# Retention and a bilinear feed-forward on one core: the last 512 rows reordered, with PSUM banks of their own and four-batch rows stored by one DMA

## The chip, the cores and the metric

The kernel runs on one core of a Trainium2 chip. That core has TensorE (PE in the profile, with its weight loads as PEld), VectorE (DVE), ScalarE (ACT), GpSimd (POOL) and SyncE (SP), and 16 DMA engines that SP, ACT and POOL can give work to. PSUM, where TensorE writes its products, is used here in banks of 128 x 512 numbers of 32 bits. The metric is the time of one execution on the device, in microseconds (us). The kernel before took 321.82 us (median of three runs, 321.82 to 322.19).

## The reference, cut to what matters

Two stages are chained. The first is a retention layer (attention with a decay instead of a softmax) over 8 batches, 8 heads, 576 positions and 64 numbers a head:

```
scores = scale * np.matmul(q, k.transpose(0, 1, 3, 2))
Dmat = np.where(rel >= 0, gamma[:, None, None] ** rel[None, :, :], 0.0)
x = np.matmul(scores * Dmat, v)      # then heads side by side: (4608, 512)
```

The second takes these 4608 rows of 512 through a bilinear feed-forward with 1536 inner columns:

```
a = x @ w_a
b = x @ w_b
out = a * b @ w_out                  # (4608, 512), float32
```

## The kernel before

The 4608 rows are cut into 18 groups of 256 (`NP = 18`), and these into blocks of 512, 256, 256 and then 512 rows. For each block `ffn_block` (L1064) runs the three products of the feed-forward: for each of 12 chunks F of 128 inner columns, four matmuls with `w_a` (L1090), a copy by ACT (`ha`, L1101), four matmuls with `w_b` (L1108) and a multiplication by DVE into `hT` (L1113). The work of the retention for later groups is spread between these matmuls from a list that is sorted by due time (`todo`); in the last block nothing of it is left.

From group 6 on the third product is not made directly. `rows_mixed` (L982) makes it by a seven-product scheme for 2 x 2 blocks (in the manner of Strassen and Winograd): the 256 rows of a group are taken as two halves, and so are the inner columns and the 512 output columns. Sums of the weights' blocks are made once (`wo_sums`); sums of the rows' blocks are made by DVE as `hT` comes (`row_sums`, L944, called after F = 7 and after F = 11). A product is six matmuls of 128 x 256, one per pair of chunks, 12 pairs of chunks halved to `NP2 = 6`. `product(g, way, ps)` issues those of one way (1 to 7), group g (0 or 1 of the block) and pairs ps. Per block that is 2 x 7 x 6 = 84 matmuls at L1009.

The results are put together like this, per group, with the lines of the profile:

- Ways 3 and 4 go to the two halves of a bank, `straights[g]`. ACT copies them to `straight` (`kept`, L1019).
- Way 1 goes to half of a bank, `both[:, g]`, which the two groups share.
- Ways 5 and 2 go to the halves of `crosses[g]`. ACT copies them to `crossed` (L1019); POOL adds `crossed` and `straight` into the two middle quarters of the group's result `osb` (L1038); DVE makes `less` = way 1 - `crossed` (L1045).
- Ways 7 and 6 are added on top of 4 and 3 in `straights[g]`; DVE adds `less` to each half, which gives the first and the last quarter of `osb` (L1054).

The order in which this is written out is the order on each engine. Before the change it is: 3 and 4 for both groups (the last pair of chunks at the end), the two copies, way 1 for both groups, ways 5 and 2 for group 0 and then for group 1, each with its copy, sum and `less`, then ways 7 and 6 for group 0 with its two additions, then the same for group 1.

A row of `osb` holds two rows of the output, so that one partition's row of 1024 numbers is 4 KB in one piece of the output. `store_mixed` (L959) issues the stores (L972). Of the twelve groups that go this way, ten lie in one batch each: one DMA of 128 partitions. Two groups (`LEFT`) are made of the last 64 positions of four batches each: four DMAs of 32 partitions, one per batch. In all blocks but the last, the stores are kept in `formed` and issued by SP when the next block has come to F = 2 (L1099). In the last block, group 0 is one of the two four-batch groups and group 1 lies in one batch. Group 1 is stored in three pieces by SP: the middle two quarters after POOL's sum, then the first and the last quarter after DVE's additions. Group 0 is stored whole, by four DMAs from ACT's queue, after its two additions.

PSUM has eight banks here: four in the pool `ps_ffn`, two in `ps_sc` and two (one tile) in `ps_o`. A new tile of a pool waits until the readers of the tile that had its place are done.

Of the kernel before, what the change touches and what calls it, by code (L numbers as in the profile page):

```python
# [10 lines left out]
FP32 = mybir.dt.float32  # L11
# [3 lines left out]
ALU = mybir.AluOpType  # L15
# [3 lines left out]
def kernel(  # L19
# [10 lines left out]
    nc = tc.nc  # L30

    B, H, S, D = q.shape
# [12 lines left out]
    NP = NTOK // 256  # L45
    LEFT = {NP - 3: 0, NP - 1: 1}
# [15 lines left out]
    def place(n):  # L62
        return n if n < NP - 2 else 2 * NP - 3 - n

    def rows_of(n):

        if n not in LEFT:
            b, m = PAIRS[n]
            return [(kp, 0, 128, b, 256 * m + 128 * kp) for kp in (0, 1)]
        return [(i // 2, 64 * (i % 2), 64, 4 * LEFT[n] + i, S - 64)  # L70
                for i in range(4)]

    def pool(name, bufs, space=None):
        kw = {} if space is None else {"space": space}
        return ctx.enter_context(tc.tile_pool(name=name, bufs=bufs, **kw))
# [13 lines left out]
    late, early = {}, ExitStack()  # L89
# [13 lines left out]
    ps_ffn = pool("ps_ffn", 4, PS)  # L103
    opening, ps_sc, ps_o = ExitStack(), {}, {}
# [94 lines left out]
    for a in (0, 1):  # L199
        nc.gpsimd.affine_select(  # L200
            out=mask_s[64 * a:64 * a + 64], in_=mask_s[64 * a:64 * a + 64],
# [58 lines left out]
    def pair_tables(step):  # L260
# [6 lines left out]
        else:  # L267
            for h in (2 * step - 2, 2 * step - 1):
# [8 lines left out]
                for n in range(FIRST)]  # L277
    second = sum_pool.tile([128, FIRST, HP, 64], FP32, tag="sums",
                           name="second")
# [28 lines left out]
    def work(budget, up_to=2):  # L308
        jobs.sort(key=lambda job: job[0])
        while jobs and jobs[0][0] <= up_to and jobs[0][1] <= budget:  # L310
            _, cost, job = jobs.pop(0)
            job()
            budget -= cost

    def pass_on(count):
        while copies_due and count:
            copies_due.pop(0)()
            count -= 1
# [610 lines left out]
    WIDE = DM // 2  # L929
# [29 lines left out]
    def store_mixed(G, osb, cols=slice(0, 2 * DM), on=nc.sync):  # L959

        n = place(G)
        for kp, r0, m, b, s0 in rows_of(n):
            if n in LEFT:
                p0 = kp * 64 + r0 // 2
                m //= 2
            elif kp == 1:
                continue
            else:
                p0, m = 0, 128
            rows = out[b * S + s0:b * S + s0 + 2 * m].rearrange(  # L970
                "(p two) c -> p (two c)", two=2)
            on.dma_start(rows[:, cols],  # L972
                              osb[p0:p0 + m].rearrange("p k c -> p (k c)")
                              [:, cols])

    formed = []

    def store_formed():
        while formed:
            store_mixed(*formed.pop(0))  # L980

    def rows_mixed(tok0, hT, sums):  # L982

        pass_on(math.inf)
        NP2 = NF // 2
        pair = [tok0 // 256 + g for g in (0, 1)]
        closing = NP - 1 in pair
        straights = [ps_ffn.tile([128, 2, WIDE], FP32, tag="ab",
                                 name=f"m34{g}") for g in (0, 1)]
        mixed = ps_o[0].tile([128, 2, 2, WIDE], FP32, tag="o", name="m15")  # L990
        apart = ps_ffn.tile([128, 2, WIDE], FP32, tag="ab", name="m52")
        both, crosses = mixed[:, 0], (mixed[:, 1], apart)

        def product(g, way, ps, begins=True):
            t0 = 256 * g
            to = {1: both[:, g], 2: crosses[g][:, 1], 3: straights[g][:, 0],
                  4: straights[g][:, 1], 5: crosses[g][:, 0],
                  6: straights[g][:, 0], 7: straights[g][:, 1]}[way]
            for p in ps:
                even, odd = 2 * p, 2 * p + 1  # L1000
                rows, cols = {
                    1: (sums[:, 0, p, g], wo_sums[:, 0, p]),
                    2: (hT[:, even, t0 + 128:t0 + 256], wo_sb[:, even, 0:WIDE]),
                    3: (hT[:, even, t0:t0 + 128], wo_sums[:, 3, p]),
                    4: (hT[:, odd, t0 + 128:t0 + 256], wo_sums[:, 4, p]),
                    5: (hT[:, odd, t0:t0 + 128], wo_sb[:, odd, WIDE:]),
                    6: (sums[:, 1, p, g], wo_sums[:, 1, p]),
                    7: (sums[:, 2, p, g], wo_sums[:, 2, p])}[way]
                nc.tensor.matmul(to, rows, cols, start=(begins and p == 0),  # L1009
                                 stop=True, skip_group_check=True)  # L1010
                yield 0.5, False

        osbs = [o_pool.tile([128, 2, DM], FP32, tag="osb", name="osb2")
                for _ in pair]
        flats = [osb.rearrange("p k m -> p (k m)") for osb in osbs]

        def kept(name, own):
            t = late[name].tile([128, 2, WIDE], FP32, tag=name, name=name)
            nc.scalar.copy(t, own)  # L1019
            return t  # L1020

        first, rest = range(NP2 - 1), (NP2 - 1,)
        for part in (first, rest):
            for g in (0, 1):
                yield from product(g, 3, part)
                yield from product(g, 4, part, False)
        kept_straight = [kept("straight", straights[g]) for g in (0, 1)]
        for part in (range(4), range(4, NP2)):
            for g in (0, 1):
                yield from product(g, 1, part, g == 0)  # L1030
        work(math.inf)
        pass_on(math.inf)
        lesses = []
        for g in (0, 1):
            yield from product(g, 5, range(NP2))
            yield from product(g, 2, range(NP2), False)
            crossed = kept("crossed", crosses[g])
            nc.gpsimd.tensor_tensor(  # L1038
                flats[g][:, WIDE:3 * WIDE].rearrange("p (k m) -> p k m", k=2),
                crossed, kept_straight[g], op=ALU.add)  # L1040
            if pair[g] == NP - 1:
                store_mixed(pair[g], osbs[g], slice(WIDE, 3 * WIDE))
            less = late["less"].tile([128, 2, WIDE], FP32, tag="less",
                                     name="less")
            nc.vector.tensor_tensor(  # L1045
                less, both[:, g].unsqueeze(1).to_broadcast([128, 2, WIDE]),
                crossed, op=ALU.subtract)
            lesses.append(less)
        for g in (0, 1):
            yield from product(g, 7, range(NP2), False)  # L1050
            yield from product(g, 6, range(NP2), False)
            for k, at, i in ((1, slice(0, WIDE), 0),
                             (0, slice(3 * WIDE, 4 * WIDE), 1)):
                nc.vector.tensor_tensor(flats[g][:, at], straights[g][:, k],  # L1054
                                        lesses[g][:, i], op=ALU.add)
                if pair[g] == NP - 1:
                    store_mixed(pair[g], osbs[g], at)
            if closing and pair[g] < NP - 1:
                store_mixed(pair[g], osbs[g], on=nc.scalar)
            elif not closing:  # L1060
                formed.append((pair[g], osbs[g]))
        yield 0, True

    def ffn_block(tb, tok0, n, runs):  # L1064
# [62 lines left out]
        if tok0 >= 256 * MIXED:  # L1127
            yield from rows_mixed(tok0, hT, sums)
            return
# [119 lines left out]
    starts, at = {}, 0.0  # L1249
# [89 lines left out]
    at = 0.0  # L1339
# [40 lines left out]
```

## Time and profile before

| what | value |
|---|---|
| median of three runs | 321.82 us |
| the profiled execution | 322.96 us, of which the span from first to last instruction is 321.0 us |
| granted TensorE clock, mean | 0.995 |
| TensorE busy | 312.6 us, 97% of the span |
| DVE, ACT, POOL busy | 62%, 45%, 49% |
| products of the last block, L1009 | 305.8 to 315.2 us |
| stores issued after 314.5 us | three by SP, four by ACT, 1.05 MB |
| the one DMA of 128 rows issued by SP at 314.6 | landed 2.2 us later |
| of the seven stores, the longest from issue to landing | 3.6 us |

The profile is one execution, and its span is counted from the first instruction. A line of a group names the source line, the engine, the operation, and `output<-inputs` with the tiles' names; a name such as SPq or ACTq is that engine's queue of instructions that issue DMAs. In the DMA answers q1 is SP's queue and q10 is ACT's. Time in the chain of waits belongs to the engine that the end of the program was waiting for at that moment.

### The profile page before, as it was taken

How to read it: one execution, taken by the hardware profiler on the slowest of the kernel's cores; microseconds unless marked ns; L12 is line 12 of the kernel's file. 1: busy time of each engine (PE TensorE's matmuls, PEld its weight loads, DVE VectorE, ACT ScalarE, POOL GpSimd, SP SyncE). 2: the span in 40 equal slices, each digit the busy share in tenths (PEclk: the TensorE clock that was granted, in tenths of full speed). 3: DMA queues.
4: the chain of work that ended last, by engine and by line, in shares of the span. 5: the costliest groups of instructions: out<-in, count | busy, mean ns of one | idle time of the engine just before them, and what ended most of it. 6: DMA issues, size and time to landing. Idle time of an engine off the chain costs nothing.

```text
span 321.0 us, 9165 instructions
## 1 busy us (share of the span) xinstructions
PE 312.6 (97%) x3799; PEld 184.3 (57%) x3799; DVE 199.7 (62%) x374; ACT 145.6 (45%) x323; POOL 155.7 (49%) x169
## 2 busy tenths in 40 slices
PE   8999999999999999999999999999999999999992
PEld 3554457768544554548554864476447744764482
DVE  4845347767758563489558854875667566744652
ACT  6745346536435463454464625553436343323330
POOL 3990078564995577573895099408950300030011
PEclk9999999999999999999999999999999999999998
DMA  8999999999989999999999979974330300030004
GB/s 213 255 200 207 256 228 193 183 209 182 196 176 221 223 218 186 233 219 261 199 251 229 172 233 157 178 170 153 73 65 2 133 3 0 2 122 11 1 0 131
DMA packets 144793, 50.92 MB, mean 159 GB/s; under 512 B 126576, under 2 KB 141680, under 8 KB 144752
## 3 DMA queue, kind: packets, MB, share of 16 engines
q1 hardware_dynamic: 138224, 44.84, 70.2%
q0 software_dynamic: 5808, 4.72, 9.4%
q10 hardware_dynamic: 720, 0.79, 0.9%
q8 instruction: 29, 0.48, 0.7%
q14 instruction: 12, 0.10, 0.1%
HBM read 37.75 MB, written 9.44 MB: 147 GB/s over the span
## 4 chain that ended last, share of the span: by engine, by line
PE 92%; DVE 4%; ACT 1%; issue 1%; DVEq 0%
PE pb L1108 29%; PE pa L1090 28%; PE m L1009 15%; PE po L1134 8%; PE w L1159 2%; PE po L913 2%; PE o L744 1%; PE sc L703 1%; PE o L731 1%; PE kv L632 1%; DVE hT L952 1%; PE tp L373 1%; DVE sums L659 1%; DVE hsum L952 1%; PE sc L391 1%
## 5 line engine op out<-in xcount | busy, mean ns | idle before, releaser
L1113 DVE TENSOR_TENSOR hT<-ha,pb 128x512 bf16<-128x512 bf16 (+1 forms) x120 | 75.7, 632 | 79.5 <-PE pb L1108 67.8
L1108 PE MATMUL pb<-xT,wb_sb 128*128 128x512 bf16 (+1 forms) x480 | 111.6, 358 | 0.1
L1090 PE MATMUL pa<-xT,wa_sb 128*128 128x512 bf16 (+1 forms) x472 | 109.9, 358 | 0.0
L1101 ACT CAST ha<-pa 128x512 bf16<-128x512 f32 (+1 forms) x120 | 64.9, 542 | 97.2 <-PE pa L1090 94.7
L1108 PEld LDWEIGHTS <-wb_sb 128*128 128x128 bf16 x480 | 46.8, 98 | 47.6 <-issue 1.9
L1090 PEld LDWEIGHTS <-wa_sb 128*128 128x128 bf16 x472 | 45.0, 98 | 43.1 <-issue 0.2
L1038 POOL TENSOR_TENSOR osb<-crossed,straight 128x512 f32<-128x512 f32 x12 | 15.2, 1271 | 102.8 <-ACT crossed L1019 95.7
L562 POOL TENSOR_TENSOR qkb<-qf,qs 64x1024 bf16<-64x1024 f32 x12 | 22.9, 1911 | 16.1 <-DMA qf<-in_q_dram 11.0
L1009 PEld LDWEIGHTS <-hT 128*128 128x128 bf16 x288 | 28.1, 98 | 4.6 <-issue 0.3
L589 POOL TENSOR_TENSOR vb<-vf,vs 128x1024 bf16<-128x1024 f32 (+1 forms) x17 | 29.1, 1713 | 3.0 <-DMA vf<-in_v_dram 1.4
L1134 PE MATMUL po<-wo_sb,hT 128*128 128x512 bf16 x120 | 27.8, 379 | 0.0
L1009 PE MATMUL m<-wo_sums,hsum 128*128 128x256 bf16 x216 | 25.5, 273 | 0.0
L567 POOL TENSOR_TENSOR qkb<-qf,qs 64x512 bf16<-64x512 f32 x24 | 24.7, 1051 | 0.7
L1009 PEld LDWEIGHTS <-hsum 128*128 128x128 bf16 x216 | 21.1, 98 | 2.4
L952 DVE TENSOR_TENSOR hsum<-hT 128x1024 bf16<-128x1024 bf16 (+1 forms) x36 | 20.5, 596 | 0.2
L578 POOL CAST qkb<-kf 64x1024 bf16<-64x1024 f32 (+1 forms) x17 | 16.6, 976 | 6.6 <-DMA kf<-in_k_dram 5.8
L712 DVE TENSOR_TENSOR sT<-sc,mask 128x512 bf16<-128x512 f32 x30 | 19.8, 681 | 0.0
L659 DVE TENSOR_TENSOR sums<-kv,sums 128x256 f32<-128x256 f32 x44 | 18.6, 422 | 1.4
L582 POOL CAST qkb<-kf 64x512 bf16<-64x512 f32 (+1 forms) x34 | 18.9, 582 | 0.9
L1134 PEld LDWEIGHTS <-hT 128*128 128x128 bf16 x120 | 11.2, 98 | 12.4
L1009 PE MATMUL m<-wo_sb,hT 128*128 128x256 bf16 x144 | 16.9, 273 | 0.1
L1009 PE MATMUL m<-wo_sums,hT 128*128 128x256 bf16 x144 | 16.7, 273 | 0.0
(111 smaller groups left out, 285.9 us busy)
## 6 DMA issues: line engine op xcount, KB each, us to landing
qf<-in_q_dram SPq DMA_DIRECT2D x32, 256.0 KB, 5.2
vf<-in_v_dram SPq DMA_DIRECT2D x32, 256.0 KB, 5.1
kf<-in_k_dram SPq DMA_DIRECT2D x31, 256.0 KB, 4.9
out_dram<-osb SPq DMA_DIRECT2D x9, 512.0 KB, 3.7
out_dram<-osb SPq DMA_DIRECT2D x18, 128.0 KB, 3.3
out_dram<-osb SPq DMA_DIRECT2D x7, 256.0 KB, 3.6
wo_sb<-in_moe_w_out_dram POOLq DMA_DIRECT2D x3, 512.0 KB, 16.0
qf<-in_q_dram SPq DMA_DIRECT2D x8, 128.0 KB, 4.1
```

The costliest lines, as they stand in the source:

```text
L562: nc.gpsimd.tensor_tensor(per_head(qkb[0:64, Q]), per_head(t[0:64]), by[0:64].unsqueeze(2).to_broadcast([64, 2 * H, D]), op=ALU.mult)
L567: nc.gpsimd.tensor_tensor(per_head(qkb[64:128, Q])[:, 1 - r::2], per_head(t[64:128])[:, r::2], by[64:128, r::2].unsqueeze(2).to_broadcast( ...
L589: nc.gpsimd.tensor_tensor(vb[:, e].rearrange("p (h d) -> p h d", d=D), t[:, e].rearrange("p (h d) -> p h d", d=D), decay[:, at], op=ALU.mult)
L659: nc.vector.tensor_tensor(sums[:, i], own, prev, op=ALU.add)
L712: nc.vector.tensor_tensor(sT[:, on].rearrange("p c k s -> p (c k) s"), sc[on].rearrange("p c k s -> p (c k) s"), mask3.unsqueeze(1).to_bro ...
L952: lambda e=e: nc.vector.tensor_tensor(*e[:3], op=e[3]))
L1009: nc.tensor.matmul(to, rows, cols, start=(begins and p == 0), stop=True, skip_group_check=True)
L1090: nc.tensor.matmul(pa[:, 0:n], wa_sb[:, c, fs], xT[:, c], start=(c == 0), stop=(c == NC - 1))
L1101: nc.scalar.copy(ha[:, 0:n], pa[:, 0:n])
L1108: nc.tensor.matmul(pb[:, 0:n], wb_sb[:, c, fs], xT[:, c], start=(c == 0), stop=(c == NC - 1))
L1113: nc.vector.tensor_tensor(hT[:, F, 0:n], has[F][:, 0:n], pb[:, 0:n], op=ALU.mult)
L1134: nc.tensor.matmul(po, hT[:, F, u * 128:(u + 1) * 128], wo_sb[:, F], start=(F == 0), stop=(F == NF - 1))
```

## The change

Three things are changed, all in the last block (`closing`) but for the last.

The order of the last block is written out anew. Ways 3 and 4 of both groups for the first four pairs, then the last two pairs of group 0 alone, ACT's copy of group 0, way 1 of group 0, the last two pairs of 3 and 4 of group 1, its copy in two halves; then the crossed ways 5 and 2 of group 0, its `less`, those of group 1; then ways 7 and 6 of group 0, its two additions and their stores; then way 1 of group 1, its `less`, way 7 with its addition and store, way 6 with its addition and store. Each `less` is made in two halves. Group 0 is stored in three pieces as group 1 is, and the pieces go to SP's and ACT's queues: the middle of group 0 on SP and of group 1 on ACT, first quarters on ACT, last quarters on SP.

The banks are laid out anew for that block: one bank for ways 3 and 4 of group 0, one each for 3 and for 4 of group 1, one each for way 1 of the two groups (in `ps_sc`), and one each for the crossed ways.

The four-batch groups are stored by one DMA whose destination has the dimensions 4 x 32 x columns, in place of four DMAs; this also holds for the other such group, one block earlier.

In the other blocks the order of the instructions is as it was, though the code is put into functions that both use.

```diff
     def store_mixed(G, osb, cols=slice(0, 2 * DM), on=nc.sync):
 
         n = place(G)
-        for kp, r0, m, b, s0 in rows_of(n):
-            if n in LEFT:
-                p0 = kp * 64 + r0 // 2
-                m //= 2
-            elif kp == 1:
-                continue
-            else:
-                p0, m = 0, 128
-            rows = out[b * S + s0:b * S + s0 + 2 * m].rearrange(
-                "(p two) c -> p (two c)", two=2)
-            on.dma_start(rows[:, cols],
-                              osb[p0:p0 + m].rearrange("p k c -> p (k c)")
-                              [:, cols])
+        b, s0 = ((4 * LEFT[n], S - 64) if n in LEFT else rows_of(n)[0][3:])
+        flat = osb.rearrange("p k c -> p (k c)")
+        if n in LEFT:
+            rows = out.rearrange("(b s two) c -> b s (two c)", b=B, two=2)[
+                b:b + 4, s0 // 2:]
+            on.dma_start(rows[:, :, cols], flat[:, cols])
+            return
+        rows = out[b * S + s0:b * S + s0 + 256].rearrange(
+            "(p two) c -> p (two c)", two=2)
+        on.dma_start(rows[:, cols], flat[:, cols])
...
+        if closing:
+            straights = [bank("m340"), [bank("m31")[0], bank("m41")[0]]]
+            both = [bank(f"m1{g}", ps_sc[0], "sc")[0] for g in (0, 1)]
+            spare = ps_o[0].tile([128, 2, 2, WIDE], FP32, tag="o", name="m521")
+            crosses = [bank("m520"), Halves(spare[:, 0])]
+        else:
+            straights = [bank(f"m34{g}") for g in (0, 1)]
+            mixed = ps_o[0].tile([128, 2, 2, WIDE], FP32, tag="o", name="m15")
+            both = [mixed[:, 0, g] for g in (0, 1)]
+            crosses = [Halves(mixed[:, 1]), bank("m52")]
...
+        def cross(g):
+            yield from product(g, 5, range(NP2))
+            yield from product(g, 2, range(NP2), False)
+            crossed[g] = kept("crossed", crosses[g].whole)
+            at = slice(WIDE, 3 * WIDE)
+            nc.gpsimd.tensor_tensor(
+                flats[g][:, at].rearrange("p (k m) -> p k m", k=2),
+                crossed[g], kept_straight[g], op=ALU.add)
+            if closing:
+                store_mixed(pair[g], osbs[g], at, nc.scalar if g else nc.sync)
...
+        def add_last(g, k, at, i):
+            nc.vector.tensor_tensor(flats[g][:, at], straights[g][k],
+                                    lesses[g][:, i], op=ALU.add)
+            if closing:
+                store_mixed(pair[g], osbs[g], at, nc.scalar if k else nc.sync)
...
+        if closing:
+            for g, ps in ((0, range(4)), (1, range(4)), (0, range(4, NP2))):
+                yield from product(g, 3, ps)
+                yield from product(g, 4, ps, g == 1)
+            kept_straight = {0: kept("straight", straights[0].whole)}
+            work(math.inf)
+            pass_on(math.inf)
+            yield from product(0, 1, range(NP2))
+            for way in (3, 4):
+                yield from product(1, way, range(4, NP2))
+            kept_straight[1] = kept("straight", *straights[1])
+            yield from cross(0)
+            lessen(0)
+            yield from cross(1)
+            for way, *end in ends:
+                yield from product(0, way, range(NP2), False)
+            for way, *end in ends:
+                add_last(0, *end)
+            yield from product(1, 1, range(NP2))
+            lessen(1)
+            for way, *end in ends:
+                yield from product(1, way, range(NP2), False)
+                add_last(1, *end)
+            yield 0, True
+            return
```

`Halves` holds a bank and its two halves; `ends` is way 7 with the first quarter and then way 6 with the last; `lessen(g)` makes `less`, in two instructions of half the width where `closing` holds.

More of the change, by code (lines that the diff above doesn't have):

```diff
@@ L987, in rows_mixed, with __init__, bank @@
         closing = NP - 1 in pair
[L988 to L992, printed above, removed]
+        class Halves(list):
+            def __init__(self, whole):
+                self.whole = whole
+                super().__init__(whole[:, k] for k in (0, 1))
+        def bank(name, place=ps_ffn, tag="ab"):
+            return Halves(place.tile([128, 2, WIDE], FP32, tag=tag, name=name))
+        if closing:
[8 more added lines that the diff above has]
+            crosses = [Halves(mixed[:, 1]), bank("m52")]
         def product(g, way, ps, begins=True):
             t0 = 256 * g
-            to = {1: both[:, g], 2: crosses[g][:, 1], 3: straights[g][:, 0],
-                  4: straights[g][:, 1], 5: crosses[g][:, 0],
-                  6: straights[g][:, 0], 7: straights[g][:, 1]}[way]
+            to = {1: both[g], 2: crosses[g][1], 3: straights[g][0],
+                  4: straights[g][1], 5: crosses[g][0],
+                  6: straights[g][0], 7: straights[g][1]}[way]
             for p in ps:
@@ L1015, in rows_mixed, with kept @@
         flats = [osb.rearrange("p k m -> p (k m)") for osb in osbs]
-        def kept(name, own):
+        def kept(name, *own):
             t = late[name].tile([128, 2, WIDE], FP32, tag=name, name=name)
-            nc.scalar.copy(t, own)
-            return t
+            width = 2 // len(own)
+            for k, part in enumerate(own):
+                nc.scalar.copy(t[:, width * k:width * k + width], part)
+            return t
+        crossed, lesses = {}, {}
+        ends = ((7, 1, slice(0, WIDE), 0), (6, 0, slice(3 * WIDE, 4 * WIDE), 1))
@@ new lines, in lessen @@
+        def lessen(g):
+            lesses[g] = late["less"].tile([128, 2, WIDE], FP32, tag="less",
+                                          name="less")
+            for ks in (slice(0, 1), slice(1, 2)) if closing else (slice(0, 2),):
+                nc.vector.tensor_tensor(
+                    lesses[g][:, ks],
+                    both[g].unsqueeze(1).to_broadcast(
+                        [128, ks.stop - ks.start, WIDE]),
+                    crossed[g][:, ks], op=ALU.subtract)
+        def add_last(g, k, at, i):
[3 more added lines that the diff above has]
+                store_mixed(pair[g], osbs[g], at, nc.scalar if k else nc.sync)
@@ L1026, in rows_mixed @@
                 yield from product(g, 4, part, False)
-        kept_straight = [kept("straight", straights[g]) for g in (0, 1)]
+        kept_straight = [kept("straight", straights[g].whole) for g in (0, 1)]
         for part in (range(4), range(4, NP2)):
@@ L1032, in rows_mixed @@
         pass_on(math.inf)
-        lesses = []
         for g in (0, 1):
[L1035 to L1048, printed above, removed]
-        for g in (0, 1):
[L1050 to L1061, printed above, removed]
+            yield from cross(g)
+            lessen(g)
+        for g in (0, 1):
+            for way, *end in ends:
+                yield from product(g, way, range(NP2), False)
+            for way, *end in ends:
+                add_last(g, *end)
+            formed.append((pair[g], osbs[g]))
         yield 0, True
```

## The prediction

> **What bounds the kernel now.** I read the page's chain of waits first, then that chain in order of time, then the last 16 us by stages and instructions, then the DMA answers for single stretches.
>
> ```profile
> PE 92%; DVE 4%; ACT 1%; issue 1%; DVEq 0%
> ```
>
> TensorE bounds the kernel; the change leaves its 84 small products in the last block and only reorders them. In order of time the chain ends so:
>
> ```profile
> 305.97 8.71 PE m L1009 x80
> 314.68 0.55 issue
> 315.24 0.42 DVE osb L1054
> ```
>
> One product is 8.71/80 = 0.109 us. By stages:
>
> ```profile
> 312.40:315.20 2.80, 2.74 (x26) 2.22 (x23) 1.60 (x4) 0.58 (x1) 2.11 (x2) 1.00 0.00 0
> 315.20:321.00 5.80, 0.00 (x0) 0.00 (x0) 0.75 (x2) 0.00 (x0) 0.00 (x0) 0.75 0.62 181
> ```
>
> The first columns are window, length, TensorE's busy time; the last three its granted clock, the DMA engines' busy share and GB/s. TensorE ends near 315.2; what follows is 5.8 us of stores. This tail is where the change acts. From the timeline, and from the stores at L972 in the same stretch:
>
> ```profile
> 311.25 0.58 ACT L1019 COPY crossed<-m 128x512 f32<-128x512 f32 x1 [1.71 <-PE m L1009]
> 311.97 2.58 POOL L1038 TENSOR_TENSOR osb<-crossed,straight 128x512 f32<-128x512 f32 x2 [27.36 <-ACT crossed L1019]
> 313.93 0.76 DVE L1054 TENSOR_TENSOR osb<-m,less 128x256 f32<-128x256 f32 x2
> 315.24 0.75 DVE L1054 TENSOR_TENSOR osb<-m,less 128x256 f32<-128x256 f32 x2 [0.55 <-issue]
> ...
> L972 ACTq DMA_DIRECT2D out_dram<-osb x4: 359/436/610, 314.8 to 316.1; - x4
> L972 SPq DMA_DIRECT2D out_dram<-osb x3: 350/350/572, 314.6 to 316.1; - x3
> DMA to landing us min/median/max: 2.2/3.1/3.6
> ```
>
> All seven stores (1.05 MB) leave after 314.5. The last, issued at 316.1, lands 3.6 us later, at 319.7; the span ends at 321.0, so 1.3 us of closing follows any last landing. Five stretches give the speed of one DMA engine: 315.40 to 316.15 (2 KB rows alone), 318.15 to 318.35 (nearly all 1 KB rows), 317.6 to 319.2 (both queues), 285.6 to 287.0 (one 128-row store of 4 KB rows) and 287.1 to 289.4 (the 32-row stores):
>
> ```profile
> q1 hardware_dynamic: 124, 0.25, 92.6%
> ...
> q1 hardware_dynamic: 59, 0.05, 75.6%
> ...
> q1 hardware_dynamic: 279, 0.25, 45.7%
> q10 hardware_dynamic: 109, 0.26, 44.8%
> ...
> q1 hardware_dynamic: 135, 0.52, 91.8%
> ...
> q1 hardware_dynamic: 183, 0.48, 78.3%
> ```
>
> Columns: packets, MB, share of 16 engines. A 2 KB row holds an engine 0.75 x 16 x 0.926 / 124 = 0.090 us, a 1 KB row about 0.2 x 16 x 0.756 / 50 = 0.048 us (some nine of the 59 packets are end marks). Both queues together: 0.51 MB in 1.6 x 16 x 0.905 = 23.2 us, 22 GB/s an engine. The last two: 25 and 17 GB/s.
>
> **The change, part by part.**
>
> *Products.* 84 before, 84 after: TensorE still ends at 315.15. What moves is who is finished after how many. Group 0's crossed pair comes after 42 products, not 48: ACT's copy at 311.25 - 6 x 0.109 = 310.60. Group 1's after 54: 311.90. Group 0 is complete after 66, at 313.2; before, after 72. The inputs made last, the halves' sums on DVE, end at 309.05; the product that needs the last of them comes near 310.3, so I cost the new order at nothing; without that cover it would cost what DVE is late, at most 0.75 us for two sums. New banks: their previous readers end by 306.8, before any product that needs them.
>
> *ACT and POOL.* Group 1's straight copy is two halves: one more instruction, under 0.58 us, in ACT's idle time before 310.6. POOL's sums keep their 1.27 us: 311.32 to 312.6 and to 313.9.
>
> *DVE.* Two `less` become four halves. Group 0's lie at 311.2 to 312.0, beside products. From 313.27: two adds (0.76) to 314.03, two halves of group 1's `less` (product 72 ends at 313.87) to 314.8, one add to 315.2, the last add 315.24 to 315.66. Before, two adds followed the last product, to 315.99: 0.33 us gained at the last issue. If DVE ran late by those two halves instead, 0.4 would be lost; I take the gain.
>
> *Stores.* ACT's four issues (0.36 to 0.61 each) go, three take their place; SP has four, not three. A: group 0's middle 256 KB on SP, 312.62. B: group 1's middle on ACT, 313.9. C: group 0's first 128 KB on ACT, queued behind B, 314.3. D: its last 128 KB on SP, 314.15. E: group 1's first on ACT, 315.3. F: its last on SP, 315.8. Nothing is behind F. The four-batch issues have no row; SP's 64-row stores (L882) bound them above, median 668 ns, its 350 here below, so 0 to 0.3 us on A; I take 0.1, since a queue idles before A. The same merge in the block before (one store at 286) has 24 us of empty SP queue behind it: nothing.
>
> *How a four-batch store is spread.* This decides. Each 32-row store left 16 end marks, so it was cut in 16 lots of two rows. All DMAs here have first dimensions of 16, 32, 64 or 128, so no row tells whether lots are cut along the first dimension both sides share or over all rows. A, C and D write 4 x 32 rows from 128 partitions. Cut along the first dimension they have four lots, on four engines; cut flat, sixteen. I take four, because every size that the trace shows splits by its first dimension and none needs a cut across two.
>
> The Trainium skill ("DMA: Bandwidth & Descriptors", section "Why a DMA increments its semaphore by 16 and not by 1") says that the engines used are the largest number up to 16 which divides the slowest dimension above one of both sides, and on these queues the lowest-numbered ones. By that rule A, C and D share the same four engines; the 16 marks per 32-row store agree, and no run here has a first dimension of four; by it the sum is the +1.5 us below, cut flat it is the first rival's time.
>
> With four lots on the same engines, each of the four carries A: 32 rows of 2 KB, C and D: 32 of 1 KB each, and of B, E and F 8 rows each: 40 x 0.090 + 80 x 0.048 = 7.4 us; at 25 GB/s for all 160 KB, 6.5. I take 7.3, what 22 GB/s with both queues gives: the nearest row. They start 0.85 us after A's issue (SP's store before: issued 314.57, traffic from 315.42) plus the 0.1: 313.6. Since C and D queue up while A runs, the engines do not idle: 320.9, and the 256 KB store's last mark came some 0.35 after its data: 321.2. Against 319.7 that is +1.5 us (bounds +0.6 at 25 GB/s; +4 at 17 GB/s, 9.6 us, a row of 16 engines reading 32 partitions, so the farther one).
>
> **Sum.** The profiled execution took 322.96 us (span 321.0, 2.0 around it), 1.1 above the median of 321.82. +1.5: span 322.5, execution 324.5, median **323.3**. Repeats differ by 0.1%; 0.2% (0.64 us) is about what can be told from no change.
>
> **Rivals.**
>
> 1. *The merged stores use all engines (or different fours).* Then A to E are nearly done when F starts. F, issued at 315.8, lands by the row of the unhindered 256 KB store (2.2) at 318.0, 1.7 us before the old last landing: **320.1**, faster. For it: the 32-row pieces, at 17 GB/s an engine, vanish, and stores start 2 us earlier. It decides as soon as the most loaded engine has under some 5.8 us of rows from 313.6 on.
> 2. *Four lots, but engines faster than the row sum.* At 25 GB/s, or with two queues overlapping, about +0.6 or less: **322.2**, no change. Against it: with both queues active the rows gave 22.
> 3. *The new order stalls TensorE* on a bank or a late sum: up to +0.75 us in the first rival, **320.9**. Readers end 2 us ahead of the products that need them, so unlikely.
>
> **Numbers.** Four lots on the same engines with the row speeds: 0.70, its own range 322.5 to 324.4 (slower starts and up to 0.9 us of gaps between the queues). Rival 2: 0.10. Rival 1, with 3 inside: 0.20. Slower by over 0.2%: 0.70, within: 0.10, faster: 0.20. The range 321.2 to 324.4 holds the first two but leaves out rival 1.
>
> **What would show it.** After: product order on TensorE unbroken to 315.2 (else rival 3); DVE's last add near 315.66; A issued at 312.6, F at 315.8. Then the DMA share falls to about 4 of 16 engines (0.25) from 313.5 to 320.8, and A, C, D carry fewer end marks; A lands 3 us or more after its issue, F about 5. If instead the share is near full for under 1 us after each issue and F lands in 2 us, rival 1 holds and the forecast is wrong.

## The result and the profile after

The changed kernel takes 325.48 us (median of six runs, 325.17 to 326.28) against 322.53 us for the kernel before in its six runs. The ratio is 1.0092, with a 95% interval of 1.0069 to 1.0116: 2.2 to 3.7 us slower. Slower was forecast, but half as much (+1.5 us, 323.3), and the range ended at 324.4. The forecast started from three of these six runs (321.82); from the median of all six, +1.5 would be 324.0 and the end of the range 325.1, so the measured time lies outside it either way.

The changed kernel's profiled execution has its products 0.58 us earlier than that of the kernel before (they begin at 305.23, there at 305.81), so its times compare after adding 0.58. The products and the additions first, from the chain of waits in order of time:

```profile
305.39 9.18 PE m L1019 x84
314.58 0.02 issue
314.60 0.42 DVE osb L1059
```

TensorE runs the 84 products without a gap, as before, and one addition follows it instead of two. It ends at 315.02, which is 315.60 on the other clock (forecast 315.66). Up to here the change does what it says. What follows has become longer; by stages (window, length, five engines' busy times, granted clock, share of the 16 DMA engines, GB/s):

```profile
314.57:316.40 1.83, 0.00 (x0) 0.00 (x0) 0.42 (x1) 0.00 (x0) 0.00 (x0) 1.00 0.60 149
316.40:318.60 2.20, 0.00 (x0) 0.00 (x0) 0.00 (x0) 0.00 (x0) 0.00 (x0) 0.61 0.80 189
318.60:322.93 4.33, 0.00 (x0) 0.00 (x0) 0.00 (x0) 0.00 (x0) 0.00 (x0) 0.50 0.28 76
322.93:323.85 0.92, 0.00 (x0) 0.00 (x0) 0.00 (x0) 0.00 (x0) 0.00 (x0) 0.50 0.00 0
```

From the last product to the end of the span it is now 9.3 us, before 5.8. In the last 4.3 us before the final landing only 0.28 of the DMA engines' time is used, that is four and a half of 16. The kernel before, cut in the same way, has no such stage:

```profile
315.14:319.70 4.56, 0.00 (x1) 0.00 (x0) 0.75 (x2) 0.00 (x0) 0.00 (x0) 0.82 0.79 230
319.70:321.00 1.30, 0.00 (x0) 0.00 (x0) 0.00 (x0) 0.00 (x0) 0.00 (x0) 0.50 0.00 0
```

The stores themselves (L967 the merged ones, L971 those of group 1), and the DMA packets from 313.05 to 322.6:

```profile
L967 SPq DMA_DIRECT2D out_dram<-osb x2: 537/552/568, 312.0 to 313.5; - x2
L967 ACTq DMA_DIRECT2D out_dram<-osb x1: 2585/2585/2585, 313.8 to 313.8; - x1
...
L971 ACTq DMA_DIRECT2D out_dram<-osb x2: 344/351/358, 313.3 to 316.5; - x2
L971 SPq DMA_DIRECT2D out_dram<-osb x1: 967/967/967, 315.1 to 315.1; - x1
DMA to landing us min/median/max: 5.8/6.5/7.0
...
DMA packets 827, 1.05 MB, mean 110 GB/s; under 512 B 59, under 2 KB 571, under 8 KB 827
```

Durations are nanoseconds, smallest, median and largest. Even group 1's plain 128-row stores, which took 2.2 us from issue to landing when unhindered before, take 5.8 to 7.0 (the line of landings is theirs). The packets under 512 B are the end marks, one from each engine that took part. Six stores on 16 engines would leave 96; three on 16 and three on four leave 60, and there are 59 in the stretch and one more at its end, at 322.61.

### The profile page after: what moved, and what is told of

The parts are those of the page before. It is cut to its first block, busy times and chain, and to the rows that moved or that the text cites. A ratio compares the mean times of both kernels' runs of the same rounds, so it can differ in the third digit from the quotient of the medians.

```text
span 323.8 us, 9132 instructions
## 1 busy us (share of the span) xinstructions
PE 308.6 (95%) x3763; PEld 184.1 (57%) x3799; DVE 199.1 (61%) x376; ACT 145.9 (45%) x324; POOL 155.6 (48%) x169
## 4 chain that ended last, share of the span: by engine, by line
PE 90%; DMA 2%; issue 1%; POOL 1%; SPq 1%; DVE 1%; ACT 0%; DVEq 0%; POOLq 0%
PE pb L1155 29%; PE pa L1137 28%; PE m L1019 17%; PE po L1181 8%; DMA vf<-in_v_dram 2%; PE po L913 2%; PE o L744 2%; PE sc L703 1%; PE o L731 1%; PE kv L632 1%; SPq L175 1%; POOL vb L365 1%; PE pa L902 1%; DVE sums L659 0%; PE tp L373 0%
## 5 line engine op out<-in xcount | busy, mean ns | idle before, releaser
L1137 PE MATMUL pa<-xT,wa_sb 128*128 128x512 bf16 (+1 forms) x448 | 106.4, 356 | 1.9 <-issue 1.1
L1181 PE MATMUL po<-wo_sb,hT 128*128 128x512 bf16 x113 | 26.7, 379 | 0.8 <-issue 0.6
L578 POOL CAST qkb<-kf 64x1024 bf16<-64x1024 f32 (+1 forms) x17 | 15.9, 937 | 7.0 <-DMA kf<-in_k_dram 6.2
L1019 PE MATMUL m<-wo_sums,hT 128*128 128x256 bf16 x144 | 16.9, 273 | 0.0
```

The source lines that it names most:

```text
L1137: nc.tensor.matmul(pa[:, 0:n], wa_sb[:, c, fs], xT[:, c], start=(c == 0), stop=(c == NC - 1))
L1181: nc.tensor.matmul(po, hT[:, F, u * 128:(u + 1) * 128], wo_sb[:, F], start=(F == 0), stop=(F == NF - 1))
```

## The experiments

A cleaner measure than the whole time is the tail, from the end of the last product to the end of the span, because the part ahead of it differs by up to 1.2 us (in one case by 3) between these executions.

| kernel | ratio to before (95% interval) | tail in the profile, us |
|---|---|---|
| before | 1 | 5.8 |
| changed | 1.0092 (1.0069 to 1.0116) | 9.3 |
| changed, four-batch stores cut in four | 0.9993 (0.9972 to 1.0014) | 5.5 |
| before, with the merged store alone | 1.0203 (1.0167 to 1.0240) | 11.9 |
| changed, batches alternating by partition | 0.9956 (0.9933 to 0.9979) | 3.8 |
| changed, group 0 stored as before | 0.9968 (0.9948 to 0.9988) | 5.0 |
| before, batches alternating, merged | 0.9956 (0.9937 to 0.9976) | 4.7 |

### The merge undone

```diff
-            on.dma_start(rows[:, :, cols], flat[:, cols])
+            for i in range(4):
+                on.dma_start(rows[i][:, cols], flat[32 * i:32 * i + 32, cols])
```

> The changed kernel with each four-batch store cut into four DMAs of 32 partitions again, on the same queues; order, banks and pieces stay. Theory (a store whose destination has first dimension four runs on four engines, and the 7.3 to 9.5 us of rows on these four engines set the end): the tail is then 12 short issues of about 0.45 us; the last one leaves SP near 316.6 on the clock of the kernel before and lands some 2.5 us later, 319.1 against 319.7: 0.4 us faster than the kernel before, 1.2 at most, 3.3 faster than the changed one. Rival (the new order, its banks, or the longer use of ACT's queue cost the time): stays within 1 us of the changed kernel, 2 to 3 us slower than before.

Measured: 0.9993, the kernel before's time again; the tail is 5.5 us. With the order, the banks and the pieces kept, undoing the merge alone takes the whole loss back, so the rival (order, banks or queues) falls. The gain of 0.4 us that I expected isn't to be seen in the times; SP's queue now carries nine issues and one of them takes long:

```profile
L968 SPq DMA_DIRECT2D out_dram<-osb x8: 314/367/1706, 312.1 to 316.8; - x8
```

so that the last store left at 317.2, which is 317.7 on the clock of the kernel before (products end at 314.62 here, there at 315.14), against the 316.6 that I had counted.

### The merge alone

In the kernel before, `store_mixed` is replaced by that of the changed kernel; nothing else.

> The kernel before with the merged four-batch store alone (old order, old banks, group 0 stored whole by one DMA from ACT). Theory: 128 KB on each of four engines, 5.2 us of rows at 25 GB/s; the same store one block earlier took 10 us from issue to landing in the changed kernel's trace, alone on its engines. Issued near 314.8, it lands between 321.2 and 324.8, with group 1's 24 rows per engine beside it up to 1 us later: 2 to 5.5 us slower than before. Rival (the merge alone costs nothing, it is the order or the pieces): within 0.6 us of the kernel before.

Measured: 1.0203, some 6.5 us slower, a little beyond the 2 to 5.5 that I gave. The whole group on four engines is worse than in pieces: its rows run from 318.66 to 327.97 by the packets' records, 9.3 us, about as long as in the changed kernel, but they start 1.0 us after the last product and not 1.3 us before it. SP's two last stores of group 1, which need the same four engines among their 16, land with it:

```profile
L971 SPq DMA_DIRECT2D out_dram<-osb x3: 332/340/1886, 317.1 to 318.7; - x3
...
DMA to landing us min/median/max: 9.7/9.8/10.0
```

(The products end at 317.7 in this execution.) The merge costs by itself and needs no new order for it.

### The same merge over sixteen engines

The rows of the four batches are made to alternate: partition 4 s + batch instead of 32 batch + s. Then 32 is the first dimension of the destination and the bytes go to the same places.

```diff
     def rows_at(n, kp):
...
+        if n in LEFT:
+            return x.rearrange("p c (k s q a) -> p q a c k s",
+                               k=2, q=2, a=2)[:, kp]
...
-            on.dma_start(rows[:, :, cols], flat[:, cols])
+            on.dma_start(rows[:, :, cols].rearrange("b s c -> s b c"),
+                         flat[:, cols])
```

> The changed kernel with the four-batch groups' rows laid out so that the four batches alternate from partition to partition (the columns of x are written in that order). The merged store then has a destination of 32 x 4 x columns: first dimensions 32 and 128, the same bytes to the same places, the same number of DMAs. Theory: sixteen lots, as the 32-row stores had; group 0's three stores are done within about 2.5 us each, the last store lands 2.2 to 2.5 us after its issue at 315.8 on the clock of the kernel before: 1.4 to 1.7 us faster than before, 4.4 faster than the changed kernel; each merged store shows 16 end marks from engines. Rival (rows scattered over four batches are slow in themselves, or the order is at fault): within 1 us of the changed kernel.

Measured: 0.9956, 0.7 to 2.2 us faster than before (1.4 to 1.7 expected), and the tail is 3.8 us, 5.5 shorter than the changed kernel's. The merged stores (L970), then the packets from 313 to 317.2:

```profile
L970 SPq DMA_DIRECT2D out_dram<-osb x2: 539/558/578, 312.2 to 313.6; - x2
...
L970 ACTq DMA_DIRECT2D out_dram<-osb x1: 659/659/659, 314.0 to 314.0; - x1
...
DMA to landing us min/median/max: 2.4/2.4/2.4
...
DMA packets 864, 1.05 MB, mean 250 GB/s; under 512 B 96, under 2 KB 608, under 8 KB 864
```

There are 96 end marks, sixteen for each of six stores, and a merged store lands in 2.4 us. The number of DMAs, their bytes, their four places in the output and the order of everything are those of the changed kernel; ACT's 2.59 us issue is gone too (0.66). So it is neither the merge nor the scattered places that cost, but the first dimension of four. (Which partition feeds which place has changed with it; the stores by themselves, below, show a like loss for a first dimension of four with nothing else in the kernel.) This kernel beats both others.

### The order alone

Group 0 is stored as before the change, by four DMAs on ACT, and group 1's end quarters both by SP:

```diff
-            if closing:
-                store_mixed(pair[g], osbs[g], at, nc.scalar if k else nc.sync)
+            if closing and g:
+                store_mixed(pair[g], osbs[g], at)
+            elif closing and not k:
+                store_mixed(pair[g], osbs[g], on=nc.scalar)
```

(and group 0's middle piece goes with the whole).

> The changed kernel's order and banks, but group 0 stored as before the change: whole, after its two additions, by four DMAs of 32 partitions on ACT's queue, now issued from 314.3 on (behind group 1's middle) instead of 314.8; group 1's end quarters both on SP, at 315.3 and 315.8 instead of 315.7 and 316.1. Theory: the order is a small gain by itself; the last landing comes 0.3 to 1 us earlier than before: 0.3 to 1 us faster. Rival (the order or the banks cost): 1 us or more slower than before.

Measured: 0.9968 (0.9948 to 0.9988), 0.4 to 1.7 us faster, with a tail of 5.0 against 5.8. The new order is a gain as long as the stores let it be one; this kernel also has its banks, and group 1's middle on ACT's queue, and what each of these is worth wasn't separated.

### The spread alone

The alternating rows and the merged store in the kernel before, with its old order.

> The kernel before (old order, old banks) with the four-batch groups' rows alternating over the batches, so that group 0 goes out whole in one DMA of 32 x 4 rows over sixteen engines. Theory (the spread over engines decides; the order is a smaller gain by itself): one store of 512 KB issued at 314.8 on the clock of the kernel before, first rows near 316, 1.3 us of rows at 25 GB/s an engine, with group 1's 256 KB beside it; the last landing near 318.5 instead of 319.7: 0.8 to 1.3 us faster than before, 0.3 to 0.8 slower than the new order with the same rows. Rival (merging is only good together with the new order): no faster than before.

Measured: 0.9956 (0.9937 to 0.9976), 0.8 to 2.0 us faster. As this was as good as the new order had been, beside another group of runs, the two were run once more side by side on one chip:

> The same kernel as interleaved, beside the old order with the same rows on the same chip: 1.1 to 1.6 us faster than before, and 0.3 to 0.9 faster than the old order, if the order is a gain by itself; if the order is worth nothing, the two are alike within 0.2 us.

> The same kernel as interleaved_old_order, beside the new order: 0.8 to 1.3 us faster than before, slower than the new order by 0.3 to 0.9 if the order is a gain by itself, by under 0.2 if it is worth nothing.

Measured together: new order 320.96 us, 0.9945 (0.9924 to 0.9967); old order 321.70 us, 0.9951 (0.9929 to 0.9973). The tails are 3.85 and 4.59 us, in the table 3.8 and 4.7, so the traces show 0.7 and 0.9 us for the new order with its pieces and queues; the intervals of the times overlap nearly wholly and don't show it. How much the order is worth in the median beside this spread stays open.

### Stores by themselves

Two kernels store zeros and nothing else, each DMA when the one before has landed. `store(p0, lots, each, apart)` stores `lots` x `each` partitions from `p0` on, to pieces `apart` rows of 4 KB from one another:

```diff
+        store(0, 1, 128, 0)
+        store(0, 4, 32, 288)
+        store(0, 4, 32, 289)
+        store(0, 4, 32, 300)
+        store(0, 4, 16, 288)
+        store(32, 4, 16, 288)
+        store(0, 4, 8, 288)
+        store(0, 2, 64, 288)
+        store(0, 1, 32, 0)
```

> Leaves the whole computation out: it only stores a tile of zeros, one DMA after another from SP, each after the one before has landed, and the series twice. In each, rows of 4 KB: 128 partitions in one piece; 4 x 32 with the pieces 288, 289 and 300 rows apart; 4 x 16 from partition 0 and from partition 32; 4 x 8; 2 x 64; 32 partitions in one piece. The question is why rows on the four engines took up to 3 times the 0.16 us of a 4 KB row in the changed kernel. Both theories: the first takes about 1.3 us of rows, the 4 x ones run on four engines, the 2 x one on two (64 x 0.16 = 10.2 us). Theory S (the source: engines that read at the same time from partitions 32 apart hinder each other): the three 4 x 32 alike, 8 to 9 us instead of 5.1; 4 x 16 from partition 0 over 2.6 us (near 4.5), from partition 32 about 2.6; 4 x 8 about 1.3. Theory D (the destination: pieces 288 rows apart collide in memory): 4 x 32 at 288 rows 8 to 9 us, at 289 and 300 rows near 5.1; 4 x 16 and 4 x 8 all slow. If all are at 5.1 and its shares, the slowness came from other traffic in the kernel.

DVE's memset waits for each landing; what it waited is in brackets, here for the first four stores and for the 2 x 64, and then the count of packets of both series:

```profile
4.97 0.91 DVE L46 MEMSET src<- 128x1024 f32 x1 [3.04 <-DMA out_dram<-src]
16.38 0.91 DVE L46 MEMSET src<- 128x1024 f32 x1 [10.50 <-DMA out_dram<-src]
27.69 0.91 DVE L46 MEMSET src<- 128x1024 f32 x1 [10.40 <-DMA out_dram<-src]
38.99 0.91 DVE L46 MEMSET src<- 128x1024 f32 x1 [10.39 <-DMA out_dram<-src]
...
70.69 0.91 DVE L46 MEMSET src<- 128x1024 f32 x1 [13.14 <-DMA out_dram<-src]
...
DMA packets 1780, 6.82 MB, mean 46 GB/s; under 512 B 116, under 2 KB 116, under 8 KB 1780
```

The 116 end marks are twice 58, and 58 is 16 for the first store, 4 for each of the six stores with a first dimension of four, 2 for the 2 x 64 and 16 for the last: a first dimension of four gives four engines, of two gives two, of 32 or 128 sixteen. That is the rule of the Trainium skill ("DMA: Bandwidth & Descriptors", section "Why a DMA increments its semaphore by 16 and not by 1"); these numbers agree with it.

The rows' own time, from the first packet's start to the last one's end in the trace: 1.43 us for the 128 rows in one piece, 8.52 for each 4 x 32 (5.1 would be 32 rows at 0.16), 3.96 and 3.38 for the two 4 x 16 (2.6), 1.73 for 4 x 8 (1.3), 11.27 for 2 x 64 (10.2). So four engines by themselves, with no other traffic, take longer than their rows would among sixteen. The distance of the pieces changes nothing: theory D falls. Theory S stands half: from partition 32 the 4 x 16 store is quicker than from 0, but not at full speed.

When in a store the time is lost, the packets show too. The 2 x 64 store in its first 3 us (58.75 to 61.75), then from there to its end (70.02):

```profile
q1 hardware_dynamic: 24, 0.10, 12.7%
...
q1 hardware_dynamic: 106, 0.43, 12.7%
```

The first 24 rows held an engine 3.0 x 16 x 0.127 / 24 = 0.25 us each, the other 104 (two of the 106 packets are end marks) 8.27 x 16 x 0.127 / 104 = 0.16 us, as among sixteen. So these engines aren't slow throughout; the store starts slowly. The first 4 x 32 store has 52 rows in its first 4.0 us and 76 in the 4.5 us after. Few engines aren't the condition either: the 32 partitions in one piece went over sixteen engines, and their rows took 0.285 us each.

The second series of stores tried theory S directly:

```diff
+        store(0, 2, 32, 288)
+        store(16, 2, 32, 288)
+        store(32, 2, 32, 288)
+        store(64, 2, 32, 288)
+        store(0, 8, 16, 288)
+        store(0, 4, 32, 288, slice(0, 512))
+        store(0, 4, 32, 288, slice(0, 256))
+        store(0, 1, 128, 0, slice(0, 256))
```

> Again only stores of zeros, each after the one before has landed, the series twice; the computation is left out. 2 x 32 rows of 4 KB from partitions 0, 16, 32 and 64 on; 8 x 16; 4 x 32 with rows of 2 KB and of 1 KB, as the changed kernel's pieces have; 128 rows of 1 KB in one piece. In the first series the four engines of a 4 x 32 store took 8.5 us instead of 5.1 at any distance of the pieces, and ended in two pairs. Theory S (engines hinder each other when they read at the same time from partitions 32 apart within one half of the partitions): 2 x 32 from 0 and from 64 take 6.5 us or more; from 32 (pairs 32 and 64) 5.1 to 5.5; from 16 between. If instead two engines alone always run at full speed, all four take 5.1 to 5.5 and the slowness needs four engines. The 4 x 32 stores: 2 KB rows 2.7 us of rows at full speed, 4.5 at the ratio of the 4 KB ones (8.5/5.1); 1 KB rows 1.5 and 2.5. 8 x 16: 2.6 at full speed.

```profile
11.39 0.91 DVE L46 MEMSET src<- 128x1024 f32 x1 [9.46 <-DMA out_dram<-src]
21.90 0.91 DVE L46 MEMSET src<- 128x1024 f32 x1 [9.61 <-DMA out_dram<-src]
31.05 0.91 DVE L46 MEMSET src<- 128x1024 f32 x1 [8.24 <-DMA out_dram<-src]
41.29 0.91 DVE L46 MEMSET src<- 128x1024 f32 x1 [9.33 <-DMA out_dram<-src]
...
55.64 0.91 DVE L46 MEMSET src<- 128x1024 f32 x1 [6.25 <-DMA out_dram<-src]
60.16 0.91 DVE L46 MEMSET src<- 128x1024 f32 x1 [3.61 <-DMA out_dram<-src]
```

(Left out are the 8 x 16 and the last store.) Rows' own time: 2 x 32 from 0, 16 and 64 takes 7.5, 7.6 and 7.5 us, from 32 it takes 6.3, where theory S said 5.1 to 5.5. Two engines are enough for the loss, and where their partitions lie matters, but partitions 32 apart are not the whole cause: the theory falls in that form, and why a store starts slowly stays open. No store here has one engine alone, so it isn't shown either that the engines hinder each other. What the case needs is the sizes: 4 x 32 with rows of 2 KB takes 4.36 us (2.9 by the row sum of the forecast), with rows of 1 KB 1.73 (1.54); 8 x 16 takes 4.30 (2.6), so even eight engines lose time.

## Why the prediction was right or wrong

**The products, the copies, the sums: right.** TensorE was unbroken, the last addition ended within 0.1 us of the forecast, and the issues came as forecast where nothing held them: A at 312.61 (312.62), B at 313.93 (313.9), D at 314.06 (314.15), F at 315.63 (315.8), with the 0.58 added.

**The spread of a four-batch store: right.** Four lots, on four engines, by the 60 end marks and the share of 0.28; and the same four each time, as the sum in the next point shows: it only comes out if all three stores lie on the same engines. The same merge with a first dimension of 32 takes the loss away and turns it into a gain.

**The rows on these four engines: mis-sized.** This is the step that failed, the "7.3 us" that the forecast took from 22 GB/s an engine, a speed shown only by stretches in which all 16 engines were busy. (160 KB are 163,840 bytes, so 22 GB/s gives 7.4 us, as the row sum does; that slip is small.) The trace has the first row at 313.24 and the last at 322.6, 9.4 us. Where the 2.1 us went, two stretches show: 313.05 to 314.65, when only A's rows move, and 319.6 to 321, when about 4.4 engines are left at work:

```profile
q1 hardware_dynamic: 16, 0.03, 24.1%
...
q10 hardware_dynamic: 81, 0.08, 16.7%
q1 hardware_dynamic: 55, 0.05, 11.0%
```

A's first 16 rows held an engine 1.6 x 16 x 0.241 / 16 = 0.39 us each, where the forecast had 0.090. The 128 rows of 1 KB in the later stretch (eight of its 136 packets are end marks) took 1.4 x 16 x 0.277 / 128 = 0.048 us each, just what the forecast had. So the speed of the rows was right once a store was under way, and what the sum lacked is a slow start. It doesn't come from the work beside it: in the kernel with the alternating rows A's rows go out while the same products run, at 0.084 us each. All 128 rows of A held the four engines 16.9 us by the packets' records, 11.5 at 0.090: 1.35 us more on each engine, the largest part of the 2.1. Why a store on these engines starts slowly stays open.

The forecast's upper bound used the slower 17 GB/s of the 32-partition stores and was set aside as the farther row; its 9.6 us came near, but whether for the same reason isn't shown. The sizes of the stores by themselves, each with its own start, give an estimate as near: A 4.36, C and D 1.73 each, and B, E and F as forecast (8 rows each, 0.72 + 0.38 + 0.38), 9.3 us. The 2.1 us, and 0.2 by which the first row was late (313.82 on the other clock, forecast 313.6), are the miss up to the landing: it came 8.4 us after the last product, forecast about 6.0, before 4.5.

**ACT's queue: not foreseen.** I gave the issue of C at most 0.67 us, the median of the 64-row stores (L882), though the longest of that same row is 1.64 us. It took 2.59, with A, B and D still unfinished on the same engines, and E, behind it on ACT, left at 317.06 on the other clock instead of 315.3. E landed last, at 322.93. It isn't shown that this added to the end: the four engines had rows to move until 322.6, and E's were among them.

**The close: 0.4 us the other way.** From the last landing to the end it was 0.92 us, before 1.3; I had kept 1.3. At the end SP goes through one wait after another, 0.06 us each: when the last store landed, one was left here, seven before.

**Together:** the landing 3.8 us later against the last product, 0.4 less to close, which is the 3.5 by which the tail grew (5.8 to 9.3); the medians show 2.95, and their interval reaches 3.7.

**The rivals.** The first (all engines) would have given 320.1. It isn't what this kernel does, but the kernel with the alternating rows is that case, and took 321.29 and 320.96 with 322.97 and 323.13 beside it: the 1.7 us that the forecast gave that case lies inside its interval. The second (engines faster than the row sum) was on the wrong side as a whole, though the median row was a little faster than forecast (0.084 and 0.046 us, forecast 0.090 and 0.048). The third (TensorE held up) did not occur.

## What to carry to other kernels

Before several DMAs are made one, look at the first dimension of both sides of the access pattern: the merged transfer is spread over the largest number of engines, up to 16, that divides both, and a batch dimension of four in front of 32 rows costs more than three issues save. Putting the long dimension first may only take another order of rows upstream, here in the columns that a copy writes. And a speed per engine that was read while all 16 run must not be used for the whole of a store on a few engines: here the first rows took one and a half to four times as long. Bound it by the slow rows as well, and let the range reach them.

## What the runs showed of the hardware that was not expected

- A store confined to few engines takes longer than its rows do among sixteen, with no other traffic: 32 rows of 4 KB an engine took 8.5 us on four engines and 7.5 on two, where 0.16 us a row among sixteen would make 5.1. The loss lies at the start (2 x 64: 0.25 us a row in the first 3 us, then 0.16). It doesn't depend on how far apart the pieces lie in memory (288, 289, 300 rows: 10.50, 10.40, 10.39 us in all) and depends in part on which partitions are read (2 x 32 from partition 32: 6.3 instead of 7.5). With 1 KB rows little of it is left (1.73 instead of 1.54).
- A queue's issue instruction can be held for long: 2.59 us for a store of 128 KB on ACT with three stores unfinished on the same four engines, 0.66 when the same stores go to all engines. Full engines may not be the only cause: with the merge undone, a 64 KB store on SP took 1.71 us to issue behind a single other store of its queue, and among the 64-row stores of the kernel before the longest is 1.64 us.
